# First queries of a second batch ahead, short first FFN tiles, unread matmuls and copies in two slots in a fused attention and FFN kernel

## The chip, the cores and the metric

The kernel runs on one core of a Trainium2 chip. The metric is the device time of one execution in microseconds (us), median of several runs. The kernel before took 455.9 us at first (3 runs, 454.5 to 456.2).

Engines: PE is TensorE (matmuls), DVE is VectorE, ACT is ScalarE, POOL is GpSimd, SP is SyncE, which only issues DMAs here.

## The reference

A causal attention with a forget gate, over 8 batches, 8 heads, 576 positions, head dimension 64, then a SwiGLU FFN over all 4608 tokens (512 to 1536 to 512). Cut to what matters:

```python
scores = q @ k.T / 8 ; cum = cumsum(log(clip(f)))
scores = where(causal, -1e9, scores + cum[:, None] - cum[None, :])
attn = softmax(scores) ; x = (attn @ v)            # tokens x 512
g = x @ w_gate ; out = (g * sigmoid(g) * (x @ w_val)) @ w_out
```

## The kernel before

The program is issued by a hand-made schedule of "slots". A head has four slots of scores (`BANKS`: the first holds queries 0 to 255, the others the rest). In a slot lie the score matmuls, the exponential on ACT, the causal select on POOL, and, three slots later, the matmuls with v. Between them FFN matmuls are poured in, paced so that a tile of tokens ends when the next becomes ready. Each engine works through its own instructions in order.

Three helpers matter. Before a pair of heads starts, its q and k are transposed on PE into one PSUM buffer (`ps_t`, a single one) and copied ("straightened") to `QK`, q by ACT and k by DVE. The same `ps_t` buffer then takes the first output of a head, so a late copy holds up PE.

```python
def transposes(p, nm):
    t = pool.tile([P, S + P - QP], BF16, name="tp", tag=tag)     # ps_t, one buffer
    for n in range(QT):
        nc.tensor.transpose(t[:, n * QP : n * QP + P], src[:, n], ident)
    for a in range(2):                                           # q on ACT, k on DVE
        ...nc.scalar.activation(dst, sr, AF.Copy) / nc.vector.tensor_copy(dst, sr)
```

The softmax sums are inverted per group of 4 heads by a chain: collect (DMA), reciprocal (DVE), back (DMA to DRAM), spread (DMA, broadcast to 64 partitions, tile `rb`), then four multiplies on DVE (`xT<-ev,rb`), which must wait for the spread:

```python
    at(s + 2, collect, g); at(s + 6, recip, g); at(s + 7, back, g); at(s + 11, spread, g)
    for j in range(GH):
        at(s + 15 + j, normalise, g * GH + j)
```

Only for batch 0, the sums are turned on PE instead, which is quick but takes PE time, and its first 256 queries of all heads go ahead, so that the FFN can begin early. The cumulative sums go into 4 extra rows of `QK` ("decay rows") by DMA.

The softmax here doesn't subtract the row's maximum and nothing guards it: scores larger than these inputs give would overflow.

## Time and profile before

| what | value | view |
|---|---|---|
| span of the profiled run | 454.3 us | page |
| PE busy | 92% | page, part 1 |
| first score matmul | 19.0 us | PE's timeline |
| second FFN tile starts (slot 37) | 72.4 us | PE's timeline |
| second full 512-token tile starts (slot 117, 1024 tokens done) | 169.6 us | PE's timeline |
| period of a 512-token tile after that | 45.57 us | PE's timeline |

The page of the kernel before: busy time, and three rows of the span in 40 slices of 11.4 us (tenths of busy time; PEclk is the granted clock of PE in tenths).

```profile
PE 418.7 (92%) x2752; PEld 239.9 (53%) x2752; DVE 290.9 (64%) x504; ACT 264.4 (58%) x537; POOL 185.0 (41%) x418
PE   2399999878799999999999999999999999999996
PEclk9999999998899999999999999999999999999999
```

From slice 12 on (125 us) PE is full. What can be won lies before that.

PE's timeline of the kernel before (start, duration, engine, line, operation, out<-in, shapes, count, and in brackets PE's idle time and who ended it):

```profile
19.04 0.80 PE L157 MATMUL s<-QK 68*128 68x256 bf16 x4 [4.58 <-DMA QK<-dec]
19.63 0.84 PE L134 MATMUL tp<-ident,b_q_97 128*128 128x128 bf16 x6
54.86 0.50 PE L134 MATMUL tp<-ident,b_q_97 128*128 128x128 bf16 x6
72.38 0.49 PE L287 MATMUL gp<-xT,wg 128*128 128x256 bf16 x3
169.58 1.03 PE L287 MATMUL gp<-xT,wg 128*128 128x512 bf16 x4
```

The first score waits for the decay rows. The six transposes take 0.84 us at 19.6 us and 0.50 us at 54.9 us; from their start to that of the next instruction it is 0.64 us against 0.34. So the early ones run at half clock, although the PEclk row says 9 there. Waits of PE between 72 and 124 us in the kernel before (who waited for whom, us in total, times, longest):

```profile
PE o_1829 L193 <- DVE ev L213: 2.3, 1, 2.3
PE o_1644 L193 <- DVE QK L141: 1.7, 1, 1.7
PE o_1598 L193 <- DVE ev L213: 1.4, 1, 1.4
```

In the full stages one wait is left per tile. DVE's timeline, then PE's, of the kernel before:

```profile
193.45 1.52 DVE L141 COPY QK<-tp 64x576 bf16<-64x576 bf16 x2
```

```profile
195.12 0.33 PE L193 MATMUL o_2860<-pt,VB_101 128*128 128x256 bf16 x2 [0.58 <-DVE QK L141]
```

PE stands 0.58 us until DVE has copied k out of `ps_t`.

### The profile page before, as it was taken

What the parts mean: (1) busy time and instruction counts of PE and PEld (TensorE: products, weight loads), DVE (VectorE), ACT (ScalarE), POOL (GpSimd) and SP (SyncE); (2) the same over time, 40 slices, a digit from 0 to 9 for tenths busy, and PEclk for the clock granted to TensorE, in tenths of its full rate; (3) what the DMA queues carried; (4) which work ended last, traced back from release to release, by engine and by line L of the source; (5) the groups of instructions that cost most, each with busy time, mean ns of one, the idle gap of its engine ahead of it and who ended that gap; (6) DMA issues with size and microseconds to landing.
All of it is one profiled execution on the core that took longest, in us unless ns stands there. A gap on an engine that the chain in (4) does not pass through costs nothing.

```text
span 454.3 us, 7863 instructions
## 1 busy us (share of the span) xinstructions
PE 418.7 (92%) x2752; PEld 239.9 (53%) x2752; DVE 290.9 (64%) x504; ACT 264.4 (58%) x537; POOL 185.0 (41%) x418
## 2 busy tenths in 40 slices
PE   2399999878799999999999999999999999999996
PEld 1266756655455555555555555555555544444442
DVE  7575655764569656965696469646964783771770
ACT  5344657786577667666766676667666631332322
POOL 6493535665535354545454545454545200000000
PEclk9999999998899999999999999999999999999999
DMA  9799935482746275628462746274614023101002
GB/s 205 188 173 216 198 76 166 107 183 62 184 105 132 56 202 132 134 54 203 130 135 56 202 131 133 56 203 130 134 28 123 26 55 98 48 0 70 24 0 95
DMA packets 68728, 52.83 MB, mean 116 GB/s; under 512 B 44624, under 2 KB 63056, under 8 KB 67728
## 3 DMA queue, kind: packets, MB, share of 16 engines
q1 hardware_dynamic: 57552, 38.35, 33.5%
q10 hardware_dynamic: 5312, 9.26, 9.4%
q0 software_dynamic: 5824, 4.72, 7.0%
q8 instruction: 22, 0.36, 0.3%
q14 instruction: 18, 0.15, 0.1%
HBM read 46.67 MB, written 10.16 MB: 125 GB/s over the span
## 4 chain that ended last, share of the span: by engine, by line
PE 68%; DVE 15%; DMA 6%; issue 4%; ACT 4%; POOL 2%; POOLq 0%; DVEq 0%; ACTq 0%
PE fo L305 18%; PE gp L287 16%; PE vp L296 15%; PE s L157 7%; DMA rb<-rc_d 4%; DVE hh L298 3%; DVE QK L141 3%; DVE xT L269 3%; DVE th L290 3%; PE tp L134 3%; ACT th L289 1%; PE rs L239 1%; ACT QK L139 1%; ACT pt L163 1%; DMA lf<-in_f_dram 1%
## 5 line engine op out<-in xcount | busy, mean ns | idle before, releaser
L163 ACT ACTIVATE pt<-s 128x384 bf16<-128x384 f32 (+2 forms) x248 | 124.0, 503 | 70.4 <-PE s L157 66.1
L175 POOL TENSOR_SCALAR_AFFINE_SELECT pt<-pt 128x256 bf16<-128x256 bf16 (+2 forms) x248 | 86.3, 350 | 171.3 <-ACT pt L163 169.5
L296 PE MATMUL vp<-xT,wv 128*128 128x512 bf16 (+1 forms) x480 | 124.2, 358 | 0.9 <-DVE th L290 0.5
L287 PE MATMUL gp<-xT,wg 128*128 128x512 bf16 (+1 forms) x480 | 124.3, 360 | 0.5 <-DVE xT L269 0.5
L290 DVE SCALAR_TENSOR_TENSOR th<-th,gp 128x512 f32<-128x512 f32 (+1 forms) x120 | 75.8, 631 | 63.6 <-ACT th L289 62.8
L305 PE MATMUL fo<-wo,hh 128*128 128x512 bf16 x432 | 107.7, 382 | 0.0
L289 ACT ACTIVATE th<-gp 128x512 f32<-128x512 f32 (+1 forms) x120 | 66.4, 554 | 56.3 <-PE gp L287 49.5
L157 PE MATMUL s<-QK 68*128 68x320 bf16 (+4 forms) x448 | 89.4, 271 | 4.6 <-DMA QK<-dec 4.6
L298 DVE TENSOR_TENSOR hh<-th,vp 128x512 bf16<-128x512 f32 (+1 forms) x120 | 75.5, 629 | 6.2 <-PE vp L296 0.9
L157 PEld LDWEIGHTS <-QK 68*128 68x128 bf16 x448 | 44.9, 101 | 46.5 <-issue 5.9
L141 DVE COPY QK<-tp 64x576 bf16<-64x576 bf16 x64 | 48.2, 753 | 29.9 <-PE tp L134 29.3
L296 PEld LDWEIGHTS <-wv 128*128 128x128 bf16 x480 | 45.3, 98 | 36.6 <-issue 2.5
L269 DVE TENSOR_TENSOR xT<-ev,rb 64x576 bf16<-64x576 f32 x56 | 45.1, 805 | 30.4 <-DMA rb<-rc_d 29.8
L287 PEld LDWEIGHTS <-wg 128*128 128x128 bf16 x480 | 44.9, 98 | 33.9 <-issue 0.7
L305 PEld LDWEIGHTS <-hh 128*128 128x128 bf16 x432 | 40.4, 98 | 35.8
L139 ACT ACTIVATE QK<-tp 64x576 bf16<-64x576 bf16 x64 | 41.2, 644 | 2.4 <-PE tp L134 1.9
L308 ACT ACTIVATE ot<-fo 128x512 f32<-128x512 f32 x36 | 21.5, 596 | 36.0 <-PE fo L305 29.7
L193 PEld LDWEIGHTS <-VB_101 128*128 128x128 bf16 x112 | 9.6, 101 | 12.8 <-PE s L157 5.7
L122 POOL CAST b_k_100<-nat_k 96x768 bf16<-96x768 f32 x16 | 16.2, 1012 | 0.0
L134 PE MATMUL tp<-ident,b_q_97 128*128 128x128 bf16 x96 | 9.0, 236 | 5.4 <-POOL b_q_97 L122 5.4
L193 PEld LDWEIGHTS <-VB_103 128*128 128x128 bf16 x112 | 9.6, 98 | 8.1 <-issue 2.4
L122 POOL CAST b_k_99<-nat_k 96x768 bf16<-96x768 f32 x16 | 13.4, 837 | 1.1 <-DMA nat_k<-in_k_dram 1.1
(344 smaller groups left out, 349.6 us busy)
## 6 DMA issues: line engine op xcount, KB each, us to landing
nat_q<-in_q_dram SPq DMA_DIRECT2D x32, 288.0 KB
nat_k<-in_k_dram SPq DMA_DIRECT2D x32, 288.0 KB
out_dram<-ot SPq DMA_DIRECT2D x36, 256.0 KB
nat_v<-in_v_dram SPq DMA_DIRECT2D x64, 128.0 KB
rb<-rc_d ACTq DMA_DIRECT2D x14, 576.0 KB
wg<-in_moe_w_gate_dram POOLq DMA_DIRECT2D x4, 384.0 KB, 7.9
wv<-in_moe_w_val_dram POOLq DMA_DIRECT2D x4, 384.0 KB, 8.6
wo<-in_moe_w_out_dram POOLq DMA_DIRECT2D x4, 384.0 KB, 6.2
```

The source lines that it names most:

```text
L139: nc.scalar.activation(dst, sr, AF.Copy)
L141: nc.vector.tensor_copy(dst, sr)
L157: nc.tensor.matmul(s[:, c : c + w], QK[b][:, 2 * j + 1, kt * P : (kt + 1) * P], QK[b][:, 2 * j, q0 : q0 + w], start=True, stop=True,)
L163: nc.scalar.activation(pt[:, off : off + c], s[:, :c], AF.Exp, scale=0.125)
L175: nc.gpsimd.affine_select(out=diag, in_=diag, pattern=[[1, m]] if m else [[0, 2], [1, P]], compare_op=ALU.is_ge, fill=0.0, base=0, channel ...
L269: nc.vector.tensor_mul(xT[a * D : (a + 1) * D, (h % H) // 2, b0 : b0 + S], E[g][:D, j], RB[g][:, j])
L287: nc.tensor.matmul(g_[:, :n], wg[:, ko, fs], xT[:, ko, ts], start=(ko == 0), stop=(ko == KD - 1))
L289: nc.scalar.activation(th[:, :n], g_[:, :n], AF.Tanh, scale=0.5)
L290: nc.vector.scalar_tensor_tensor(out=th[:, :n], in0=th[:, :n], scalar=1.0, in1=g_[:, :n], op0=ALU.add, op1=ALU.mult)
L296: nc.tensor.matmul(v_[:, :n], wv[:, ko, fs], xT[:, ko, ts], start=(ko == 0), stop=(ko == KD - 1))
L298: nc.vector.tensor_mul(h_[:, :n], th[:, :n], v_[:, :n])
L305: nc.tensor.matmul(o[:m], hh[fc][:, m0 : m0 + m], wo[:, fc, :], start=(fc == 0), stop=(fc == KF - 1))
```

## The change

Its intent: start earlier and fill the thin first stages. It has five parts. (1) `QK` becomes four tiles, pair 0's decay rows are sent at once, the other pairs' go through DRAM. (2) 36 unread matmuls of 512 columns keep PE busy, so that its clock rises. (3) Batch 0's second halves no longer turn on PE but take the DMA chain. (4) Batch 1's first queries go ahead too, its inputs are loaded early, and the FFN starts with tiles of 256, 256, 256 and 384 tokens, ends with 384. (5) q and k are copied in two slots, with the transposes a slot earlier. The core of the diff:

```diff
+AHEAD = 2
-    QKA = consts.tile([KR, NBUF, 4, NB * P], BF16, name="QK")
+    QK = [consts.tile([KR, 4, NB * P], BF16, name=f"QK{i}") for i in range(NBUF)]
+    def idle(n):
+        for _ in range(n):
+            z = ps_ffn.tile([P, MT], F32, name="z", tag="f")
+            nc.tensor.matmul(z, ident, ident.unsqueeze(1).to_broadcast([P, MT // P, P]), start=True, stop=True)
-        ahead = h < H and i == 0
+        ahead = h < AHEAD * H and i == 0
-    TILES = [(0, QSPLIT), (QSPLIT, MT - QSPLIT)] + [(t0, MT) for t0 in range(MT, N_TOK, MT)]
+    TILES = [(0, QSPLIT), (QSPLIT, QSPLIT), (2 * QSPLIT, QSPLIT), (3 * QSPLIT, AHEAD * S - 3 * QSPLIT)]
+    TILES += [(t0, min(MT, N_TOK - t0)) for t0 in range(AHEAD * S, N_TOK, MT)]
 ... startup: idle(9), idle(2), idle(7), idle(4), idle(6) between the transposes; then
+        for r in range(4):
+            (nc.scalar if r < 2 else nc.sync).dma_start(
+                out=QK[0][D + r : D + r + 1, :, :S], in_=dec[0:2, :, r])
+        nc.sync.dma_start(out=dec_dram[:H], in_=dec[:H])
 ... rows(1), rows(2), rows(3) from DRAM; turn()/turn_back() for first halves only
-            at(s0 - 11, cast, p, "q"); at(s0 - 7, cast, p, "k")
-            at(s0 - 7, transposes, p, "q"); at(s0 - 3, transposes, p, "k")
+            cq, tq, ck, tk, cv = s0 - 12, s0 - 8, s0 - 8, s0 - 4, s0 - 4
+            for a in range(2):
+                at(t + a, straighten, p, nm, a, nc.scalar if nm == "q" else nc.vector)
+    for n in range(H):
+        at(n, idle, 1)
```

## The prediction

> **What bounds the kernel now.** The page's busy table: PE 418.7 of 454.3 us (92%), DVE 64%, ACT 58%, POOL 41%. The 40 slices put the loss at the front; PE's timeline gives it piece by piece:
> - 0 to 19.04 us: the first score matmul waits for the decay rows (DMA QK<-dec, 15.96 to 18.8), though they were computed at 12.0 (DVE L359). The DMA goes out only after a k copy (DVE L141), as all four QK buffers are one tile.
> - 19 to 38 us: PE is cold. Six 128-column transposes take 0.64 us start to start, later 0.335. The Trainium skill, "TensorE: Matmul & The Clock Gate", Part 1, says that the array starts at half clock until about 3.4 us of sustained work; the trace agrees, though the page's clock column shows full speed. Cost, an estimate: 9 us. POOL is dense too, 20.1 to 31.5 us (selects 0.54, casts 0.82, weight issues 0.76).
> - 72 to 124 us (scheduler slots 37 to 85): one 256-token FFN tile is spread over 48 slots; warm matmul work is about 36 of 52 us. The rest: PE waits for PSUM held by q/k copies (0.3 and 0.6 us, once 1.75), for DVE ev while DVE waits for rb<-rc_d (1.4 and 2.3), and two cold spells.
> - From 124 us PE is 97 to 100% busy: work there is only moved.
>
> **What the change does.**
> 1. QK in four tiles, pair 0's rows sent at once: first scores near 14.5 us, -4.5. Pairs 1 to 3 go through DRAM, perhaps 1 us late.
> 2. 36 unread 512-column matmuls: 28 lie in waiting time, 8 cost 0.21 us each (1.7). PE is warm for slots 8 to 14: -3.5 us. Slots 0 to 7 stay POOL-bound (11.4 us).
> 3. Batch 0's second halves leave the PE turns (0.24 + 0.49 us, 8 heads): -5.9 us of PE; two DMA chains more.
> 4. Batch 1's first queries early, tiles of 256, 256, 256, 384: by slot 117 the FFN has done 1152 tokens, not 1024 (7.7 us at 59.9 ns a token), and slots 37 to 85 get work. The largest part: of about 16 us lost I expect two thirds back. The extra tile costs under 1 us.
> 5. Copies in two slots, transposes a slot earlier: the 0.3 and 0.6 us waits mostly go, about 3 us.
>
> Sum of warm PE work (an estimate): slot 8 at 27 us, 51 at 60, 62 at 80, 83 at 105, 117 at 143, if nothing waits. Against it: weights (2 us a piece at 200 GB/s), four pairs' inputs and early normalising DMAs crowd into 13 to 55 us, where DMA is already full: +3. Waits for rb and sc, as slots are shorter than these DMAs: +4. Latency where FFN is thin (slots 12 to 51): +3. So slot 117 near 153 us, before 169.6 (second full 512 tile, PE L287). The rest, 285 us before, loses 7.7 and about 1: 277.
>
> **Predicted: 430 us**, 8 in 10 between 420 and 442. Faster by over 2%: 0.93; within: 0.06; slower: 0.01.
>
> **Right if** PE's timeline shows first scores near 14.5 us, transposes at 0.33 us before 25 us, PE over 90% from 50 us on, and the tile at token 1152 starting near 153 us. **Wrong if** DVE or POOL wait for nat, wo, sc or rb DMAs between 30 and 65 us for over 8 us, if the unread matmuls, sharing PSUM buffers with scores and turns, stall PE in slots 0 to 7, or if PE goes cold near 100 us.

## The result

The changed kernel took 461.3 us (4 runs, 460.2 to 461.7), the kernel before on the same chips 456.0 us (454.5 to 456.5). The ratio is 1.0118, 95% interval 1.0088 to 1.0148: slower by 1.2%, which is under the 2% from which the study calls a kernel slower, but clear of the noise. Ratios here are the mean time of one kernel's fast runs over that of the other's in the same rounds, so not quite the ratio of the medians quoted.

The page of the changed kernel, the same rows:

```profile
PE 423.2 (92%) x2836; PEld 250.4 (55%) x2836; DVE 294.2 (64%) x523; ACT 268.4 (58%) x551; POOL 179.1 (39%) x425
PE   6689769799899799989998999899989999999996
PEclk9878989899899989999999999999999999999999
```

PE is busier at the very start (the unread matmuls), but has holes up to slice 28, once per tile. PE's timeline of the changed kernel:

```profile
13.72 0.49 PE L135 MATMUL tp<-ident,b_k_103 128*128 128x128 bf16 x6 [3.73 <-ACT QK_96 L142]
14.06 2.46 PE L150 MATMUL z<-ident 128*128 128x512 bf16 x6
16.31 0.53 PE L166 MATMUL s<-QK_96 68*128 68x256 bf16 x2
27.99 0.63 PE L243 MATMUL rs<-ident_f,rcp 128*64 128x128 f32 x2 [1.06 <-DVE rcp L238]
29.58 0.64 PE L166 MATMUL s<-QK_96 68*128 68x320 bf16 x2
60.93 0.33 PE L166 MATMUL s<-QK_96 68*128 68x256 bf16 x2 [2.69 <-ACT pt L172]
62.06 0.53 PE L202 MATMUL o_972<-pt,VB_107 128*128 128x320 bf16 x2 [0.80 <-DVE ev L223]
81.00 0.38 PE L297 MATMUL gp<-xT,wg 128*128 128x256 bf16 x2
84.06 0.27 PE L297 MATMUL gp<-xT,wg 128*128 128x256 bf16 x1 [2.68 <-DVE xT L278]
178.40 1.02 PE L297 MATMUL gp<-xT,wg 128*128 128x512 bf16 x4
```

Six unread matmuls (`z`) lie right before the first score. They take 0.38 us each from start to start, where warm ones take 0.22: PE had stood for 3.73 us before and ran at half rate again until about 17.8 us. Slot 8 (the first 320-column score) comes at 29.6 us, the second FFN tile (slot 51) at 81.0, slot 117 at 178.4 with 1152 tokens done. To compare: the kernel before reached slot 117 at 169.6 with 1024 tokens, and 128 tokens of FFN take 7.7 us on PE (59.9 ns a token), so it was at the same point at about 177.3. All the gain of the first 178 us is gone, and after it the tile period is 46.54 us instead of 45.57.

The long link in the chain of waits of the changed kernel between 40 and 70 us (start, us, what):

```profile
43.68 16.23 DMA nat_v<-in_v_dram
```

An input of batch 1 (v of the third pair) takes 16 us to land; POOL, ACT and then PE stand for it at 58 to 61 us. And the pair of lines from the full stages, DVE, then PE:

```profile
201.19 1.52 DVE L278 TENSOR_TENSOR xT<-ev,rb 64x576 bf16<-64x576 f32 x1
202.73 0.75 DVE L144 COPY QK_97<-tp 64x576 bf16<-64x576 bf16 x1
203.40 0.67 DVE L308 TENSOR_TENSOR hh<-th,vp 128x512 bf16<-128x512 f32 x1
204.08 0.76 DVE L144 COPY QK_97<-tp 64x576 bf16<-64x576 bf16 x1
```

```profile
204.90 0.34 PE L202 MATMUL o_3101<-pt,VB_104 128*128 128x256 bf16 x2 [1.53 <-DVE QK_97 L144]
```

The k copy now stands behind a normalising multiply, and its second half behind another FFN step too. PE waits 1.53 us where it waited 0.58. (This multiply took 1.52 us, twice as long as most; POOL ran casts meanwhile. Whether the one made the other was not tested.)

The landing times of the weight DMAs, from the tile views: `wo` took 6.2 us in the median before, 13.7 us after; `wg` 7.9 and 12.6. The early inputs of batch 1 share the DMA engines with them. From 29 to 51 us DMA is as full in both kernels (windows view, a share of 1.27 before and 1.24 after); from 51 to 71 us it is 0.55 before and 0.73 after.

### The profile page after: what moved, and what is told of

The parts are those of the page before. It is cut to its first block, busy times and chain, and to the rows that moved or that the text cites. A ratio compares the mean times of both kernels' runs of the same rounds, so it can differ in the third digit from the quotient of the medians.

```text
span 459.3 us, 8077 instructions
## 1 busy us (share of the span) xinstructions
PE 423.2 (92%) x2836; PEld 250.4 (55%) x2836; DVE 294.2 (64%) x523; ACT 268.4 (58%) x551; POOL 179.1 (39%) x425
## 4 chain that ended last, share of the span: by engine, by line
PE 69%; DVE 12%; DMA 10%; issue 4%; ACT 2%; POOL 1%; SPq 1%; ACTq 0%; DVEq 0%; POOLq 0%
PE fo L315 18%; PE gp L297 16%; PE vp L306 15%; PE s L166 7%; DMA nat_v<-in_v_dram 5%; DMA rb<-rc_d 4%; PE tp L135 3%; DVE xT L278 3%; DVE hh L308 3%; DVE th L300 3%; DVE QK_97 L144 2%; DMA nat_q<-in_q_dram 1%; DVE ev L223 1%; SPq L98 1%; ACT th L299 1%
## 5 line engine op out<-in xcount | busy, mean ns | idle before, releaser
L184 POOL TENSOR_SCALAR_AFFINE_SELECT pt<-pt 128x256 bf16<-128x256 bf16 (+2 forms) x240 | 79.7, 333 | 185.3 <-ACT pt L172 184.2
L297 PE MATMUL gp<-xT,wg 128*128 128x512 bf16 (+2 forms) x528 | 127.4, 346 | 5.1 <-DVE xT L278 4.0
L306 PE MATMUL vp<-xT,wv 128*128 128x512 bf16 (+2 forms) x528 | 128.2, 346 | 0.9 <-DVE hh L308 0.9
L300 DVE SCALAR_TENSOR_TENSOR th<-th,gp 128x512 f32<-128x512 f32 (+2 forms) x132 | 77.7, 589 | 74.6 <-ACT th L299 72.5
L299 ACT ACTIVATE th<-gp 128x512 f32<-128x512 f32 (+2 forms) x132 | 68.4, 518 | 54.1 <-PE gp L297 44.2
L308 DVE TENSOR_TENSOR hh<-th,vp 128x512 bf16<-128x512 f32 (+2 forms) x132 | 77.2, 585 | 9.1 <-PE vp L306 1.7
L278 DVE TENSOR_TENSOR xT<-ev,rb 64x576 bf16<-64x576 f32 (+2 forms) x72 | 52.5, 729 | 35.4 <-DMA rb<-rc_d 34.2
L166 PE MATMUL s<-QK_96 68*128 68x320 bf16 (+4 forms) x112 | 23.3, 280 | 2.7 <-ACT pt L172 2.7
L166 PE MATMUL s<-QK_97 68*128 68x320 bf16 (+4 forms) x112 | 22.4, 270 | 0.4 <-DMA QK_97<-dec_d 0.3
L166 PE MATMUL s<-QK_98 68*128 68x320 bf16 (+4 forms) x112 | 21.8, 264 | 0.0
L166 PE MATMUL s<-QK_99 68*128 68x320 bf16 (+4 forms) x112 | 21.5, 261 | 0.0
L166 PEld LDWEIGHTS <-QK_96 68*128 68x128 bf16 x112 | 11.6, 105 | 13.2 <-issue 4.0
L202 PEld LDWEIGHTS <-VB_104 128*128 128x128 bf16 x112 | 9.8, 102 | 16.0 <-DVE QK_97 L144 11.2
L166 PEld LDWEIGHTS <-QK_97 68*128 68x128 bf16 x112 | 11.4, 103 | 12.7 <-issue 2.3
L144 DVE COPY QK_98<-tp 64x576 bf16<-64x576 bf16 x16 | 12.0, 749 | 8.9 <-PE tp L135 8.7
L166 PEld LDWEIGHTS <-QK_99 68*128 68x128 bf16 x112 | 11.0, 98 | 10.5
## 6 DMA issues: line engine op xcount, KB each, us to landing
wg<-in_moe_w_gate_dram POOLq DMA_DIRECT2D x4, 384.0 KB, 12.6
wo<-in_moe_w_out_dram POOLq DMA_DIRECT2D x4, 384.0 KB, 13.7
```

The source lines that it names most:

```text
L144: eng.tensor_copy(dst, sr)
L166: nc.tensor.matmul(s[:, c : c + w], QK[b][:, 2 * j + 1, kt * P : (kt + 1) * P], QK[b][:, 2 * j, q0 : q0 + w], start=True, stop=True,)
L184: nc.gpsimd.affine_select(out=diag, in_=diag, pattern=[[1, m]] if m else [[0, 2], [1, P]], compare_op=ALU.is_ge, fill=0.0, base=0, channel ...
L278: nc.vector.tensor_mul(xT[a * D : (a + 1) * D, (h % H) // 2, b0 : b0 + n], E[g][:D, c : c + n], RB[x][:, j * n : (j + 1) * n])
L297: nc.tensor.matmul(g_[:, :n], wg[:, ko, fs], xT[:, ko, ts], start=(ko == 0), stop=(ko == KD - 1))
L299: nc.scalar.activation(th[:, :n], g_[:, :n], AF.Tanh, scale=0.5)
```

## The experiments

Where no other is named, the base of an experiment is the changed kernel. "Before" runs lay at medians of 455.3 to 456.6 us. Unless said otherwise, the result was correct. Where a stage is compared, it is one profile of each kernel.

### First call: the suspected costs one by one

**a1_no_unread.**

```diff
-        for _ in range(n):      # idle()
+        for _ in range(0):
```

> The changed kernel without its 36 unread matmuls. Theory 'unread matmuls pay' (the prediction): slots 0 to 14 run cold again, 2 to 4 us slower than the changed kernel (463 to 465 us). Rival 'they stand in the way': six of them lie between the last transposes (13.7 us) and the first score (16.3 us), so the first score comes at about 14.3 us, and as the clock falls back at 28 us anyway, the time is equal or up to 3 us shorter (458 to 461).

Measured: 458.6 us, ratio to before 1.0060 (1.0020 to 1.0101). The first score came at 15.3 us, a microsecond earlier, and the first FFN matmul at 35.4 (35.7 with them). So the unread matmuls gave nothing; whether they cost is less clear, for the intervals just meet.

**a2_one_slot.**

```diff
-            cq, tq, ck, tk, cv = s0 - 12, s0 - 8, s0 - 8, s0 - 4, s0 - 4
+            cq, tq, ck, tk, cv = s0 - 11, s0 - 7, s0 - 7, s0 - 3, s0 - 4
-                at(t + a, straighten, ...)
+                at(t, straighten, ...)
```

> The changed kernel with both q/k copies in one slot and the transposes at the old slots, from batch 2 on. The waits of PE for a q/k copy (o <- DVE QK L144) were 1.5 us once per batch after, 0.6 before. Theory 'two slots made this wait longer': the waits go back to about 0.6 us and the stretch from 178 us on gets 3 to 5 us shorter (about 457 us). Rival 'the waits come from the normalising DMA ahead of the copies on DVE': unchanged within 1 us.

Measured: 455.4 us, ratio 0.9958 (0.9909 to 1.0008; one slow run, 459.3, left out of the ratio). The tile period is 45.57 us again, to the hundredth what it was before; the four tile periods after slot 117 save 0.97 us each, 3.9 us. This part of the change is shown to cost, and it is the largest single cost: the profiled span grew by 5.0 us in all (454.3 to 459.3).

In this kernel PE stayed warm after the unread matmuls (in the profiled run), slot 8 came at 28.3 us and the first FFN matmul at 32.5 us. Its startup is that of the changed kernel, instruction by instruction, so it was chance, or something that these runs don't show, that PE went cold there and not here. But the next one waited for a weight, and the second tile began at 79.7 us, against 81.0 in the changed kernel: of the 3.2 us at the first FFN matmul 1.3 were kept.

**a3_half_w and b3_half_w** (wrong results; the second is the kernel before with the same edit).

```diff
-  nc.gpsimd.dma_start(out=t[:, :, lo:hi], in_=src[:, :, lo:hi])
+  nc.gpsimd.dma_start(out=t[:, : KD // 2, lo:hi], in_=src[:, : KD // 2, lo:hi])
-  nc.gpsimd.dma_start(out=t[:, lo:hi], in_=src[:, lo:hi])
+  nc.gpsimd.dma_start(out=t[:, lo:hi, : DM // 2], in_=src[:, lo:hi, : DM // 2])
   ... the matmuls read wg[:, ko % 2], wv[:, ko % 2], and wo's first half twice
```

> Wrong result on purpose: the changed kernel, each weight DMA with half the bytes, the same number of instructions on every engine. Theory 'DMA is full until 60 us and slots 8 to 51 wait for inputs': the wait for nat_v near 58 us goes, slot 51 (end of the first FFN tile, 81 us) comes 8 us or more earlier, total 450 us or less. Rival 'in-order waits between engines and the cold clock, not bytes': less than 4 us shorter (457 us or more).

> Wrong result on purpose: the kernel before with the same halved weight DMAs. If the bytes are what the early batch 1 runs into, the kernel before gains little: 0 to 3 us (453 to 456). If the bytes limit both kernels alike, it gains as much as the changed one.

Measured: the changed kernel 453.8 us (ratio of fast runs 0.9925, 0.9861 to 0.9989; the profiled run was a slow one, 459.1), the kernel before 455.7 us (0.9994). The wait for `nat_v` near 58 us is gone and the second tile starts at 76.9 us, not 81.0. So the bytes matter to the changed kernel and not to the one before: about 4 us at slot 51, half of what the DMA theory wanted, and 2.4 us at slot 117 (176.0 us). The total lies between the marks of the two theories (450 and 457 us): the three fast runs took 450.8, 451.5 and 456.1 us.

### Second call: parts together, and parts alone

**c1_both_undone** is a1 and a2 together. **c2_turns** gives back to it the PE turns of batch 0's second halves:

```diff
-            if h < H and i == 0:
+            if h < H and i in (0, NSLOT - 1):
+                half = 0 if i == 0 else 1
-                at(s + 1, turn, h); at(s + 2, turn_back, h)
+                at(s + 1, turn, h, half); at(s + 2, turn_back, h, half)
```

**c3_ahead1** takes from c1 the early queries and the short tiles (`AHEAD = 1`, `TILES` as before). **b1_start** is the kernel before with the startup of the change only, without unread matmuls.

> The changed kernel without the unread matmuls and with the q/k copies in one slot at the old slots. If the two costs found singly (2.7 and 6 us) add up: 452 to 454 us. If they overlap: 455 to 456. The period of the 512-token tiles must be 45.6 us as before, not 46.5.

> As c1_both_undone, and batch 0's second halves normalised by PE turns as before the change, so that the second FFN tile can begin at slot 37, not 51. Theory 'the DMA chain of the second halves starves PE: the first tile is thinned over slots 12 to 51': the second tile starts 15 us or more earlier, the tile at token 1152 6 us or more earlier, total 446 us or less. Rival 'a slot costs its 1.1 us whatever FFN work lies in it, and the turns cost 5.9 us of PE': equal to c1_both_undone within 2 us or slower.

> As c1_both_undone, but batch 1's first queries not ahead, and the FFN tiles of before. What stays of the change is the startup and the DMA chain for batch 0's second halves. If the early queries and short tiles help by themselves: 3 us or more slower than c1_both_undone (456 or more). If they only move the thin stretch: within 2 us of it.

> The kernel before with the startup of the change alone (four QK tiles, pair 0's rows sent at once, the other pairs' through DRAM, new load order), no unread matmuls. Theory 'the earlier first score is kept': first score near 15.3 us instead of 19.0, total 3 us shorter (452 to 453). Rival 'it is lost at the weights, which bound the first FFN tile': the first FFN matmul at 37 us as before, total 455 to 456.

| kernel | us | ratio to before (95%) | first score | second tile | 1152 tokens done (1024 plus 7.7) |
|---|---|---|---|---|---|
| before | 455.3 | 1 | 19.0 | 72.4 | 177.3 |
| changed | 461.3 | 1.0118 (1.0088 to 1.0148) | 16.3 | 81.0 | 178.4 |
| c1_both_undone | 454.1 | 0.9983 (0.9922 to 1.0045) | 15.0 | 82.2 | 173.7 |
| c2_turns | 453.7 | 0.9957 (0.9889 to 1.0024) | 14.9 | 76.4 | 176.8 |
| c3_ahead1 | 452.9 | 0.9960 (0.9908 to 1.0013) | 15.4 | 80.1 | 173.3 |
| b1_start | 453.6 | 0.9973 (0.9922 to 1.0025) | 14.4 | 72.4 | 174.4 |

The four do not differ from each other beyond their scatter, so the costs of a1 and a2 did not add up (c1 is where a2 was, though its 454.1 us lies between the two marks that I had set). What they say is this: with or without the early queries and short tiles (c1 against c3), with turns on PE or through DMA (c1 against c2), the same work is done at about the same time. My theory that the thin first tile starves PE wanted the second tile 15 us earlier in c2 and 446 us in all; it came 6 us earlier, and the gain was lost again by token 1152. That theory falls.

The startup (b1_start) shows how an early start is lost. PE's timeline of its scores:

```profile
14.44 0.84 PE L165 MATMUL s<-QK 68*128 68x256 bf16 x4
18.53 0.48 PE L165 MATMUL s<-QK 68*128 68x256 bf16 x2 [1.05 <-DMA QK<-dec_d]
19.76 0.52 PE L165 MATMUL s<-QK 68*128 68x256 bf16 x2
```

Pair 0's two heads start at 14.4 us, 4.6 us earlier than before; pair 1 waits until 18.5 for its rows from DRAM (it started at 20.3 before). Slot 8 comes at 30.2 instead of 31.3.

### Third call: what a slot costs, and where a copy may stand

**d1_ffn_last**: c1_both_undone, with all FFN matmuls issued after the attention.

```diff
-        while nxt is not None and s >= begin(nxt[0]):
+        while nxt is not None and s < 0:
```

> As c1_both_undone, but the whole FFN is issued after the last attention slot (a measurement, far slower in all). It shows what a slot of attention costs when PE has nothing else. By PE work alone a slot would be 0.42 us, by ACT or POOL 0.65. Theory 'a slot has a floor of about 1 us from the engines waiting for one another, so a stretch thin in FFN work costs its slots times the floor': 0.9 to 1.1 us a slot, in slots 8 to 51 as well as later. Rival 'inputs: DMA bounds the first 60 us only': below 0.8 us a slot after 70 us, and 1.2 in slots 8 to 40.

Measured (one run, state unknown): 603.6 us, as meant only for its slots. Sixteen slots (four heads) take 17.04 us in most of the kernel, so 1.065 us a slot, and there the clock was 0.50. The windows view of d1 (stretch, length, busy time and count of PE, PEld, DVE, ACT, POOL, then PEclk, DMA share, GB/s):

```profile
140.00:160.00 20.00, 17.19 (x100) 11.34 (x99) 8.51 (x15) 13.60 (x28) 12.72 (x30) 0.50 0.65 140
```

No engine is full, yet nothing goes faster. At half clock the PE work of a slot is twice 0.42 us (an estimate), so this alone does not tell a cold PE from waits; g1 below does.

**f1_early_tp**: c1_both_undone, with the transposes a slot earlier as in the change, but both copies in that slot.

> As c1_both_undone, but with the casts and transposes one slot earlier, as the change has them, and both q/k copies in that one slot. One look: the period of the 512-token tiles, which was 45.57 us with copies in one slot at the old slots and 46.54 with the change. If the spreading of the copies makes the 1 us: 45.6. If the earlier slot makes it (the k copy then meets the last normalising multiply): 46.2 or more.

Measured (one run, state unknown): 459.4 us, tile period 46.70 us. So the spreading is not the cost; the earlier slot is. DVE's timeline of f1, then PE's:

```profile
199.08 1.26 DVE L278 TENSOR_TENSOR xT<-ev,rb 64x576 bf16<-64x576 f32 x1
200.35 1.52 DVE L144 COPY QK<-tp 64x576 bf16<-64x576 bf16 x2
```

```profile
201.93 0.34 PE L202 MATMUL o<-pt,VB 128*128 128x256 bf16 x2 [1.41 <-DVE QK L144]
```

The k copy of slot 4 (of 16) falls into the slot of the last of the four multiplies, which stand in slots 1 to 4. In slot 5 (c1_both_undone) PE waits only 0.58 us, as in the kernel before.

**e2_b1_late_norm** and **e3_c2_late_norm**: b1_start and c2_turns with the multiplies 8 slots after the spread instead of 4, so that DVE needn't wait for `rb`. (I had also tried this edit on c1_both_undone; it deadlocked.)

```diff
-                at(s + 15 + j, normalise, g * GH + j)
+                at(s + 19 + j, normalise, g * GH + j)
```

> As b1_start, with the normalising multiplies 8 slots after the spread DMA instead of 4. DVE waits 3.5 to 4 us for rb once or twice per tile; with it PE waits for evictions and copies behind. Theory 'DVE standing at the rb DMA is what makes slots 37 to 85 long': the 512-token tile at token 512 starts 4 us or more earlier than in b1_start (121.3 us), and the tile period falls from 45.57 by 0.3 to 0.6 us; total 447 to 450 us. Rival 'the wait is slack': within 1.5 us of b1_start (453.6).

> As c2_turns (PE turns for both halves of batch 0, batch 1 ahead, short tiles), with the normalising multiplies 8 slots after the spread DMA. If the rb waits are what hides the gain of the early queries: at least 3 us below c2_turns (450 us or less). If the early inputs on a full DMA are: within 2 us of c2_turns (452 to 455).

Measured: 463.5 us (ratio 1.0174, 1.0139 to 1.0208) and 459.7 us (1.0080, 1.0024 to 1.0136): misses of both theories. DVE's wait for `rb` between 60 and 440 us fell to 2.3 us in e2, and still the tile period rose to 47.6 us. The multiplies had been moved into slots 5 to 8 of 16. I took the k copy in slot 5 for the cause, but the trace names another: PE's long wait, 1.54 us once per tile, ends with the q copy on ACT. DVE, ACT and PE of e2, in order of time:

```profile
241.80 1.41 DVE L277 TENSOR_TENSOR xT<-ev,rb 64x576 bf16<-64x576 f32 x1
243.24 0.27 DVE L262 RECIPROCAL rc<-sc 128x18 f32<-128x18 f32 x1
243.53 0.32 ACTq L265 DMA_DIRECT2D rc_d<-rc  x1
243.90 1.30 ACT L141 ACTIVATE QK<-tp 64x576 bf16<-64x576 bf16 x2 [2.44 <-PE s L165]
245.26 0.34 PE L201 MATMUL o<-pt,VB 128*128 128x256 bf16 x2 [1.54 <-ACT QK L141]
```

The next group's reciprocal (slot 8) stands on DVE behind the last multiply; ACT, which issues the DMA `back` in slot 9, stands until the reciprocal is there; and the q copy is behind that issue on ACT. (The view puts ACT's 2.44 us down to PE's scores, but the q copy needs only the transposes, and these ended at 241.3.) The k copy of slot 5 was late too, but PE lost little there. Taking away the long wait for `rb` made the kernel slower, because of what the multiplies now stood in front of.

### Fourth call: telling the last ones apart

**g1_warm**: d1_ffn_last with two unread matmuls in each slot. **g2_warm_two**: g1 with two buffers each in `ps_t` and `ps_o` (from `ps_ffn`).

```diff
-    for n in range(H):
-        at(n, idle, 1)
+    for n in range(NSLOT * BH):
+        at(n, idle, 2)
```

> As d1_ffn_last (all FFN after the attention), with two unread 512-column matmuls in every attention slot and none at the start. In d1_ffn_last a slot took 1.06 us, but with the clock at 0.50. PE work in a slot is here 0.42 + 0.43 us at the warm rate. Theory 'the floor of a slot is engines waiting for one another': with a warm clock still 1.0 to 1.15 us a slot. Rival 'the floor was the cold clock': 0.85 to 0.92 us a slot.

> As g1_warm, with two PSUM buffers each for attention output and for transposes/first halves instead of one (taken from the FFN, which is not running). If the single buffers make the floor: at least 0.1 us a slot less than g1_warm. If not: within 0.05 us of it.

Measured in the slots (one run each, state unknown; in all 603.1 and 672.8 us): g1 17.04 us for 16 slots on average, 1.065 each, the same as d1; g2 15.55 us, 0.97 each. The windows view of g1:

```profile
160.00:180.00 20.00, 17.35 (x136) 10.45 (x136) 8.80 (x15) 13.78 (x30) 12.33 (x29) 1.00 0.56 123
```

At full clock, with 0.85 us of PE work (an estimate), a slot still takes 1.065 us. By this view PE is idle for 2.65 of 20 us, 0.14 us a slot. Waits of PE in g1 between 80 and 280 us:

```profile
PE o L202 <- POOL pt L184: 16.5, 18, 1.6
PE o L202 <- DVE ev L223: 6.4, 10, 1.5
PE o L202 <- DVE QK L144: 3.6, 3, 1.7
```

Second buffers take off 0.09 us, a little less than the 0.1 that I had set as the mark. But the average hides a lump. The four heads of 16 slots take 3.7, 4.0, 3.7 and 5.4 to 6.2 us (first scores of g1, 122 to 276 us), and the last holds one wait of 1.5 to 1.7 us. DVE's timeline of g1, then PE's:

```profile
203.04 2.71 DVE L278 TENSOR_TENSOR xT<-ev,rb 64x576 bf16<-64x576 f32 x3
205.78 1.52 DVE L144 COPY QK<-tp 64x576 bf16<-64x576 bf16 x2
```

```profile
207.44 0.33 PE L202 MATMUL o<-pt,VB 128*128 128x256 bf16 x2 [1.55 <-POOL pt L184]
```

The k copy ends at 207.30, POOL's select at 207.34, so the view names POOL. The copy stands behind the multiplies, and DVE had stood 3.3 us before the first of them (here the view names a copy on ACT; 11 other such waits between 80 and 280 us are for the spread, 31.8 us). In g2 one wait of 1.1 to 1.3 us is left in every 16 slots, for the same k copy. So there is no price that every thin slot pays: most of the waits are this one meeting on DVE. The other heads take 3.7 or 4.0 us, about what heads take in the kernel before between 73 and 99 us (3.7 us, 0.92 us a slot, PE busy for 0.80 of it). In d1, at half clock, all heads take 4.25 us; that its average equals that of g1 is chance.

**h1_b1_norm5**: b1_start with the multiplies 9 slots after the spread (`s + 20 + j`), in slots 6 to 9 of 16. **h2_b1_direct**: b1_start with pair 1's rows sent from SBUF too.

```diff
         for r in range(4):
+            for p in range(2):
-                out=QK[0][D + r : D + r + 1, :, :S], in_=dec[0:2, :, r]
+                out=QK[p][D + r : D + r + 1, :, :S], in_=dec[2 * p : 2 * p + 2, :, r]
-        rows(1)
```

> As b1_start, with the normalising multiplies 9 slots after the spread DMA: slots 6 to 9 of 16, clear of the k copies in slots 5 and 13. With 8 slots they met the k copy and the period of the 512-token tiles rose from 45.6 to 47.6 us. Theory 'it is the meeting with the k copy on DVE that costs': the period falls to 45.0 to 45.6, total 449 to 454 us. Rival 'any later multiply costs': 47 us or more, total above 460.

> As b1_start, with pair 1's decay rows sent straight from SBUF like pair 0's. In b1_start the first score came at 14.4 us, but slot 2 waited for pair 1's rows until 18.5, and slot 8 came at 30.2 (31.25 before). If that wait is what ate the early start: slot 2 near 16, slot 8 near 28 and the total 2 us shorter than b1_start (451.5). If POOL, dense from there on, or the weights bound slot 8: total within 1 us of b1_start.

Measured: h1 451.4 us, ratio 0.9911 (0.9864 to 0.9957), tile period 45.17 us (45.57 before). One slot later than e2 turns a loss of 1.7% into a gain of 0.9%: the place of the multiplies in DVE's queue is what costs. Four periods make 1.6 us of the gain; the last two tiles, 34.18 and 31.08 us in place of 35.86 and 31.74, make 2.3. h2 456.5 us, ratio 1.0008 (0.9970 to 1.0046): a miss; the first score came at 16.1 us, later than in b1, pair 1 at 18.9, no sooner than in b1, and slot 8 at 30.0. So the edit did not bring what it was meant to test.

### Fifth call: the repaired versions

**k1_c1_norm5** and **k2_c3_norm5**: c1_both_undone (early queries, short tiles) and c3_ahead1 (neither), both with the multiplies of whole groups 9 slots after the spread.

```diff
-            free = sp + 4 + (j if n == S else j // 2)
+            free = sp + (9 + j if n == S else 4 + j // 2)
```

> c1_both_undone (early batch 1 queries, short tiles, neither unread matmuls nor copies in two slots) with the multiplies of the whole groups 9 slots after the spread DMA, as in h1_b1_norm5. If the early queries and short tiles give something once the multiplies are out of the way: below h1_b1_norm5, 449 us or less. If they give nothing: c1_both_undone less the 2 us of the shorter tile period (45.2 for 45.6 us), 452 us, level with h1_b1_norm5 (451.4) within 1.5 us.

> c3_ahead1 (no early batch 1 queries, the tiles of before, batch 0's second halves through DMA) with the same later multiplies. Expected 450 to 451 us, the best of all; against k1_c1_norm5 it shows once more what the early queries and short tiles give: nothing if within 1.5 us of it or below it.

Measured, 6 runs each on one chip: k1 454.7 us, ratio 0.9970 (0.9927 to 1.0014); k2 450.5 us, ratio 0.9853 (0.9809 to 0.9897; one slow run left out). k2 is faster than both kernels of this case, by 1.5% against the one before. DVE's timeline of k2 in the full stages, and PE's:

```profile
206.10 1.52 DVE L144 COPY QK<-tp 64x576 bf16<-64x576 bf16 x2 [3.95 <-PE tp L135]
208.07 2.29 DVE L278 TENSOR_TENSOR xT<-ev,rb 64x576 bf16<-64x576 f32 x3
```

```profile
208.29 0.33 PE L202 MATMUL o<-pt,VB 128*128 128x256 bf16 x2
```

Now the copy comes first, the multiplies after it, and PE has no wait in brackets. The early queries and short tiles, in k1, cost 1.2% against k2. There the tile at token 1152 began at 181.5 us, against 173.7 in c1: that tile becomes ready five slots later, and the tile before it is stretched to fit. This reading of k1 is argued, not tested.

## Why the prediction was wrong

It said 430 us, between 420 and 442, and faster with 0.93. The time was 461.3 us. Point by point:

1. *First score near 14.5 us, -4.5 us.* It came at 16.3. Six of the unread matmuls, 2.25 us until the first score starts, stood in its way (in a1 it came at 15.3). And the gain was not kept: in b1_start pair 1 ran 4.1 us after the first score ("perhaps 1 us late" was mis-sized), and slot 8 was 1.1 us earlier than before, not 4.5. What bounds slot 8 stays open: in h1, with the startup of b1, it came at 28.6 us, where b1 has one more wait of PE, 1.16 us for DVE's reciprocal, and POOL was busy for 5.9 of the 6 us from 20 to 26 us in both the changed kernel and b1.
2. *The unread matmuls make PE warm for slots 8 to 14: -3.5 us.* The transposes did run at the warm rate before 25 us, as predicted. But PE was cold from 14.1 to 17.8 us, after its wait of 3.73 us, and again after a gap of 1.06 us at 28 us; the granted clock from 29 to 39 us was 0.54. (The prediction also took the trace for agreeing with the page: in the kernel before PE stayed at half rate for 18 us of nearly continuous work, see the last section.) The page of the Trainium skill that the prediction leaned on, "TensorE: Matmul & The Clock Gate" (HAM oscillation), sets the harmful gap at about 3.4 us of idle PE; here 7.4 busy us in the 10 us around it (20 to 30 us), and gaps of 1 us, were followed by half clock. a1 without them was no slower. In a2, where PE stayed warm, slot 8 and slot 51 each came 1.3 us earlier than in the changed kernel: where the clock stayed up PE's work did get shorter. But 1.3 us is no more than equal startups scatter (slot 8 at 30.2 us in b1 and 28.6 in h1).
3. *Leaving the PE turns saves 5.9 us.* With the turns back (c2) the time did not change: 453.7 against 454.1 us. But c2 also lets the second tile begin 14 slots earlier, so two effects may cancel there. That PE time saved in a stretch where PE waits is no time saved, is argued and not shown.
4. *Early queries and short tiles, two thirds of 16 us back.* This is the largest wrong term. c1 against c3, and k1 against k2, show no gain, and in k1 a loss. The step that failed is the "sum of warm PE work": slots 8 to 51 as 33 us of PE work. They took 51.4 us (29.6 to 81.0). The profile names most of the 18: 8.2 us of PE waits (the list of waits from 28 to 82 us, less the one at 28; 2.7 of it are for `nat_v`), and 6.3 us of lost clock (10 us at 0.54 and 8 us at 0.79); some 4 us stay unassigned. Slots 51 to 117 took 97.4 us and not 83: PE was idle for 7.9 us, 3.4 of it for multiplies that had waited for `rb`, and the clock was 0.95, some 4.9 us. I had allowed 10 us of waits for all stages together and no cold clock at all; the stages up to slot 117 ran 35 us over the sum. By the schedule the change didn't remove thin slots, it moved them from slots 37 to 85 to slots 8 to 51. That this is why nothing was won is argued: c2, which may start the second tile at slot 37 again, won nothing either.
5. *Copies in two slots, the 0.3 and 0.6 us waits mostly go, 3 us.* The sign was wrong. The 0.58 us became 1.53 us; the tile period grew by 0.97 us, 3.9 us in four periods, and f1 shows that the earlier slot did it. The prediction looked at PE's wait and not at what else stood in DVE's queue in the new slot.
6. *DMA +3 us.* Of the right kind: the weights landed 13 us instead of 6 to 8 after issue, and `nat_v` came after 16 us. Batch 1's inputs are only a part of that: without them, in c3, the weights took 10.6 to 11.2 us (in b1 6.1 to 9.8). By a3 the weights' bytes cost about 4 us at slot 51, which is not in addition to point 4. Of the list under "wrong if", this one came true in part: POOL stood 3.5 us and ACT 4.2 us for `nat_v`. PE also went cold, from 86 to 89 us. Of the signs under "right if" only the warm transposes came: from 51 to 71 us PE was busy for 71%.

In sum: slot 117 at 178.4 us instead of 153 (25 us), and the rest 281 us instead of 277 (4 us, the copies). The first part is named from the profile, term by term; only the copies are shown by experiment.

## What to carry to other kernels

Summing one engine's work gives a floor and not a schedule: where stages are thin, measure what a step costs with the filler taken out (as g1_warm did), look at the waits one by one before you trust their average, and ask whether a change removes thin steps or only moves them. Before you move an instruction on an in-order engine to shorten a wait, look at what already stands in its new place: one slot on DVE made 0.97 us per tile here, and 9 slots instead of 8 turned +1.7% into -0.9%. Follow the chain over all queues: in e2 a multiply on DVE held a DMA issue on ACT, and that held PE. A long wait can cost little (h1 has 29 us less of DVE's waits for `rb` than b1 and is some 2 us faster), and a short one (PE for a copy, 0.6 us) costs in full; the one to shorten is the one on the full engine.

## What the Trainium skill lacked or had wrong

- "TensorE: Matmul & The Clock Gate", Part 1: about 3.4 us of sustained work is said to raise the clock. In the kernel before PE was busy for 19.0 of 20 us between 20 and 40 us, by the windows view, and its matmuls stayed at the half rate (0.64 us from start to start for six transposes, 0.335 later) until the FFN matmuls began at 37.4 us. Much of that work was transposes, some of them in fp32; the rival that they don't count as busy (third point) was not tested. 9 unread 512-column matmuls did raise the clock (3.4 us), as the page says. It lacks a figure for how busy is busy enough.
- The same page, HAM oscillation: gaps over about 3.4 us are named as harmful. In the changed kernel one of 3.73 us was followed by half rate, as the page says, but so were gaps of 1.06, of 2.69 plus 0.80, and of 2.68 plus 0.74 us (there the half rate came at 86 us, a microsecond after the last gap). The page's next section does tell of short idles after which the clock swings; it has no length for them. That the gaps were the cause is not shown: a2, with gaps up to 0.77 us between 18 and 30 us, stayed warm.
- The same page says that the full clock "doesn't engage" for transposes, which do not count as busy in the same way. Once warm, six 128x128 transposes here took 0.335 us from start to start, 56 ns each, half of their cold time: so they run at the full clock when other matmuls have raised it. Whether they can raise it themselves was not tested.
- The same page warns that clock events in traces have been unreliable; how that looks in a profile's clock row, it does not say. Here the row showed full speed for the first 38 us of the kernel before, while the durations were those of half clock. Mean clocks of two kernels (0.992 before, 0.969 after) can therefore not be compared; durations can.
